# Linear attention and two MLPs on one core: q times kv in the four quarters of the PE array, maximum of k on POOL

## The chip, the cores and the metric

The kernel runs as one program on one core of a Trainium2 chip. The metric is the device time of one execution in microseconds (us). The engines are named as the profile names them: PE is the matrix engine (its weight loads stand apart as PEld), DVE the vector engine, ACT the scalar engine, POOL the general engine, SP the engine whose queue issues all transfers of this kernel.

## What is computed

The cut reference; there are 8 batches of 8 heads, 576 tokens each, head size 64, so 4608 tokens of 512 numbers enter the MLPs.

```python
q_s = exp(q - max(q, axis=-1)); q_s = q_s / (sum(q_s, axis=-1) + 1e-09)
k_s = exp(k - max(k, axis=2));  k_s = k_s / (sum(k_s, axis=2) + 1e-09)   # axis 2: tokens
kv  = einsum('bhsd,bhse->bhde', k_s, v)                # 64 x 64 for each head
x   = einsum('bhsd,bhde->bhse', q_s, kv)               # then heads side by side
x   = relu(x @ w_in)**2 @ w_out                        # 512 -> 2048 -> 512
out = (sigmoid(x @ w_gate) * (x @ w_val)) @ w_out2     # 512 -> 1536 -> 512
```

## The kernel before

All numbers are float32. The products of the MLPs are made of three float32r matmuls each (`mm3`, lines 216 to 219: high by high, high by low, low by high); these three lines are most of PE's work. Blocks 0 and 1 of 512 tokens go through the first MLP in the plain form (`conv_stage`), while the weights are read, split and stored; the later blocks go in pairs, with seven products in place of eight (`plan_seven`), through `in_stage` (first MLP) and `gate_stage` (second MLP).

The attention runs beside the MLPs, as small pieces between the matmuls of a stage. It handles two heads at a time, so there are 4 head pairs `p`. Its work has two parts.

For each batch `b` and pair `p` (`plan_k`): `k` and `v` are loaded with the tokens on the partitions (5 groups of 128). DVE takes the maximum over the 5 groups (`k_max`). What is left is a maximum over 128 partitions. It is made in four steps: PE transposes the 128 x 128 tile (`k_turn`, line 404), DVE reduces it to a column (`k_diag`, line 410), ACT puts the column on a diagonal (`k_put`, line 415), and PE multiplies ones by the diagonal, so that every partition has the row of maxima in PSUM (`k_all`, line 420). DVE subtracts it (`k_sub`, line 425), ACT takes the exponential (`k_exp`, line 429), PE multiplies by `v` and by a column of ones (`k_mm`, line 443: for each group and head a matmul of 128 rows and 64 columns of the array, so the two heads take the two column halves), DVE makes the reciprocal (`k_rec`), and ACT copies the two scaled 64 x 64 blocks onto the diagonal of a 128 x 128 tile `kvf` (`k_copy`, line 460).

For each block `j` of 512 tokens and pair `p` (`plan_q`): `q` is loaded, and its softmax over 64 numbers is made. From block 2 on, `q` lies in memory with blocks of 32 x 32 turned, a maximum or sum over 64 is put together with a small PE matmul (`q_swap`, line 502), and DVE turns the blocks (`q_turn`). Then PE multiplies by `kvf` (`q_mm`, line 571): one matmul over all 128 rows and columns for each batch that the block touches (one or two, `segs`). Each float32 matmul stands as two instructions in the trace. ACT copies the result out of PSUM (`x_copy`).

PSUM has 8 banks: 6 belong to the MLPs (`bank0` to `bank5`), 2 to the attention (the tag `pa`). `k_turn` takes one of them and `k_copy` gives it back; `q_swap` and `q_mm` take one each.

The order of every engine's instructions is fixed before the run. `Plan.trace` is a small simulator: each operation has a key (its wanted time), a cost on an engine, the operations it comes after, the buffers it takes and gives, and some have a `slack` that offers them later than they are ready. An engine takes the ready operation of the lowest key, and its instructions are issued in that order. A result is taken to be usable 0.15 us after its end on DVE, ACT and POOL, 0.2 us on PE. The attention's PE steps of blocks and batches above 3 have a slack of 2.5 us, those below none. Each engine then runs its list in order and waits on semaphores, so an operation that takes longer than its cost in the plan holds up what stands behind it on the engines that wait.

`plan_blocks` lays the attention of blocks 2 and 3 beside the plain stage of block 1, that of blocks 4 and 5 beside the first `in_stage`, that of 6 and 7 beside the second `gate_stage`, and that of block 8 beside the third `in_stage`.

Of the kernel before, what the change touches and what calls it, by code (L numbers as in the profile page):

```python
# [10 lines left out]
F32 = mybir.dt.float32  # L11
# [4 lines left out]
AF = mybir.ActivationFunctionType  # L16
# [7 lines left out]
DMA, PE, ACT, DVE, POOL, FREE = "DMA PE ACT DVE POOL FREE".split()  # L24
# [5 lines left out]
class Plan:  # L30
# [13 lines left out]
    def add(self, key, engines, name, fn, *args, after=(), take=(), give=(), slack=0.0):  # L44
        n = len(self.ops)
        assert name not in self.names, name
        self.names[name] = n
        self.ops.append((key, n, engines, name, fn, args, tuple(after), tuple(take), tuple(give), slack))
# [95 lines left out]
def attention_mlp_mlp(  # L144
# [20 lines left out]
    nc = tc.nc  # L165
    NB, NP, _, N = q.shape
    NBATCH, _, _, RK, D2 = k.shape
    D = D2 // 2
    NT, DM = out.shape
    S = NT // NBATCH  # L170
# [3 lines left out]
    F2 = w_out2.shape[0]  # L174
    wide = w_in.dtype == I64

    SIZES = {"X": 14, "W": 10, "S": 6, "f": 19, "x": 8, "q": 3, "a": 6, "w": 5, "k": 2, "v": 2, "km": 1, "kr": 2, "pa": 2, "qm": 4, "qr": 4}
    cst = ctx.enter_context(tc.tile_pool(name="cst", bufs=1))
    p4 = ctx.enter_context(tc.tile_pool(name="p4", bufs=1))
    p2 = ctx.enter_context(tc.tile_pool(name="p2", bufs=1))  # L180
# [10 lines left out]
    kvf = [[cst.tile([128, 128], F32, name=f"kv{a}{p}") for p in range(NP)] for a in range(2)]  # L191

    vts = [cst.tile([128, RK, 2 * D + 3], F32, name=f"vt{i}") for i in range(SIZES["v"])]
    banks = [pu.tile([128, N], F32, name=f"bank{i}") for i in range(6)]

    plan = Plan(SIZES)
    add = plan.add
# [12 lines left out]
    def hi_of(dst, src):  # L210
        nc.scalar.activation(out=dst, in_=src, func=AF.Copy)  # L211
# [158 lines left out]
    kmx = {}  # L370
    kps = {}
# [45 lines left out]

    def k_all(b, p):

        nc.tensor.matmul(kps[b, p][:, KM0:KM0 + 2 * D], ones, kmx.pop((b, p)), start=True, stop=True)  # L420

    def k_sub(b, p):
        kt = kt_t[b, p]
        mx = kps[b, p][:, KM0:KM0 + 2 * D].rearrange("p (o c) -> p o c", o=1)
        nc.vector.tensor_tensor(out=kt, in0=kt, in1=mx.to_broadcast([128, RK, 2 * D]), op=ALU.subtract)

    def k_exp(b, p):
# [2 lines left out]

    def k_mm(b, p):
        kt, vt = kt_t.pop((b, p)), vt_t.pop((b, p))
        ps = kps[b, p]
        for r in range(RK):
            if b == 0:
                nc.tensor.matmul(ps[:, 0:2 * D + 1], kt[:, r, :], vt[:, r, 0:2 * D + 1], start=(r == 0), stop=(r == RK - 1))  # L436
                continue

            for h in range(2):
                rows = slice(D * h, D * h + D)  # L440
                c = (D + 1) * h
                o = D * (1 - h)
                nc.tensor.matmul(  # L443
                    ps[rows, o:o + D + 1], kt[:, r, rows], vt[:, r, c:c + D + 1],
                    start=(r == 0), stop=(r == RK - 1), skip_group_check=True,
                )
# [8 lines left out]
    def k_copy(b, p):  # L455
        ps, ri = kps.pop((b, p)), kmx.pop((b, p))
        for h in range(2):
            s = slice(D * h, D * h + D)
            c = slice((D + 1) * (1 - h), (D + 1) * (1 - h) + D) if b else s
            nc.scalar.activation(out=kvf[b % 2][p][s, s], in_=ps[s, c], func=AF.Copy, scale=ri[s])  # L460

    def segs(j):
        done = 0
        while done < N:
            b, s = divmod(j * N + done, S)
            c = min(N - done, S - s)
            yield slice(done, done + c), b
            done += c
# [8 lines left out]

    def q_load(j, p):
        t = tile2("q", "qt")
        nc.sync.dma_start(out=t, in_=q[j, p])  # L480
        q_t[j, p] = t

    def qu_cols(j):
# [83 lines left out]
    def q_mm(j, p):  # L567
        t = q_ps.pop((j, p))
        ps = pa.tile([128, N], F32, tag="pa", name="xps")
        for e, b in segs(j):  # L570
            nc.tensor.matmul(ps[:, e], kvf[b % 2][p], t[:, e], start=True, stop=True)  # L571
        q_ps[j, p] = ps
# [10 lines left out]

    def x_copy(j, p):
        t = tile2("x", "xf")
        hi_of(t, q_ps.pop((j, p)))
        x_t[j, p] = t


# [5 lines left out]
    def plan_k(b, p, key, step, wait=()):  # L595
        n = (b, p)
        big = ("W", "W") if b == 0 else ("k", "v")
        bank = [] if b == 0 else ["pa"]
        add(key - 5 if b else p, {DMA: 0.92}, ("kt",) + n, k_load, b, p, after=wait, take=big[:1])
        add(key - 4 if b else p + 4, {DMA: 0.92}, ("vt",) + n, v_load, b, p, after=wait, take=big[1:])  # L600
        add(key, {DVE: 1.02}, ("kmx",) + n, k_max, b, p, after=[("kt",) + n], take=["km"])
        add(key + 0.5 * step, {PE: 0.3}, ("kt2",) + n, k_turn, b, p, after=[("kmx",) + n], take=bank, slack=slack(b))
        add(key + step, {DVE: 0.29}, ("kdr",) + n, k_diag, b, p, after=[("kt2",) + n])
        add(key + 1.2 * step, {ACT: 0.33}, ("kdg",) + n, k_put, b, p, after=[("kdr",) + n])
        add(key + 1.5 * step, {PE: 0.4}, ("kgm",) + n, k_all, b, p, after=[("kdg",) + n], give=["km"], slack=slack(b))
        add(key + 2 * step, {DVE: 0.85}, ("ks",) + n, k_sub, b, p, after=[("kgm",) + n])
        add(key + 3 * step, {ACT: 0.75}, ("ke",) + n, k_exp, b, p, after=[("ks",) + n])
        add(key + 4 * step, {PE: 0.8 if b else 1.3}, ("kp",) + n, k_mm, b, p, after=[("ke",) + n, ("vt",) + n], give=big, slack=slack(b))
        add(key + 5 * step, {DVE: 0.31}, ("kr",) + n, k_rec, b, p, after=[("kp",) + n], take=["kr"])
        add(  # L610
            key + 6 * step, {ACT: 0.65}, ("kv",) + n, k_copy, b, p,
            after=[("kr",) + n] + (kv_users[b - 2, p] or [("kv", b - 2, p)] if b > 1 else []), give=["kr"] + bank,
        )

    def plan_q(j, p, key, step, qmul):
        n = (j, p)
        pe = j < NPE
        add(key - 5 if j else p + 0.1, {DMA: 0.73}, ("qt",) + n, q_load, j, p, after=x_before.get(j, []), take=["q"])
        add(key, {DVE: 0.69}, ("qa",) + n, q_red, j, p, ALU.max, "qm", after=[("qt",) + n], take=["qm"])
        if not pe:  # L620
            add(key + 0.3 * step, {PE: 0.15}, ("qaw",) + n, q_swap, j, p, after=[("qa",) + n], take=["pa"], slack=slack(j))
        if j == JACT:
            add(key + 0.5 * step, {DVE: 0.15}, ("qs",) + n, q_neg, j, p, after=[("qa",) + n])
        else:
            add(key + 0.5 * step, {DVE: 0.7 if pe else 0.86}, ("qs",) + n, q_sub, j, p, after=[("qa" if pe else "qaw",) + n], give=["qm"] if pe else ["qm", "pa"])
        add(key + step, {ACT: 2.4 if j == JACT else 0.63}, ("qe",) + n, q_exp, j, p, after=[("qs",) + n], give=["qm"] if j == JACT else [])
        add(key + 2 * step, {DVE: 0.69}, ("qb",) + n, q_red, j, p, ALU.add, "qr", after=[("qe",) + n], take=["qr"])
        if not pe:
            add(key + 2.3 * step, {PE: 0.15}, ("qbw",) + n, q_swap, j, p, after=[("qb",) + n], take=["pa"], slack=slack(j))
        add(key + 2.5 * step, {DVE: 0.36 if pe else 0.58}, ("qr",) + n, q_sum, j, p, after=[("qb" if pe else "qbw",) + n], give=[] if pe else ["pa"])  # L630
        if j == JACT:
            qmul = {ACT: 2.4}
        add(key + 3 * step, qmul, ("qm",) + n, q_mul, j, p, CHOSEN, after=[("qr",) + n], give=["qr"])
        if pe:
            add(key + 4 * step, {PE: 0.5}, ("qT",) + n, q_turn_pe, j, p, after=[("qm",) + n], take=["pa"], give=["q"], slack=slack(j))
        else:
            add(key + 4 * step, {DVE: 0.72}, ("qT",) + n, q_turn, j, p, after=[("qm",) + n], take=["a"], give=["q"])
        if pe:
            add(key + 5 * step, {ACT: 0.6}, ("qh",) + n, q_copy, j, p, after=[("qT",) + n], take=["a"], give=["pa"])
        bs = [b for _, b in segs(j)]  # L640
        add(
            key + 7 * step, {PE: 1.0}, ("xp",) + n, q_mm, j, p, after=[("qh" if pe else "qT",) + n] + [("kv", b, p) for b in bs],
            take=["pa"], give=["a"], slack=slack(j),
        )
        for b in bs:
            kv_users[b, p].append(("xp",) + n)
        if pe:
            add(key + 8 * step, {ACT: 0.6}, ("xh",) + n, x_hi, j, p, after=[("xp",) + n], take=["SX"[j]])
            add(key + 9 * step, {DVE: 0.7}, ("x",) + n, x_lo, j, p, after=[("xh",) + n], give=["pa"])
            return  # L650
        add(key + 8 * step, {ACT: 0.6}, ("x",) + n, x_copy, j, p, after=[("xp",) + n], take=["x"], give=["pa"])

# [623 lines left out]
```

## Time and profile before

| | |
|---|---|
| median of 3 runs | 1712.5 us (1712.0 to 1712.92) |
| the profiled execution | 1716.37 us, its span 1714.6 us |
| PE busy | 1661.7 us (97% of the span) |
| DVE busy | 1138.8 us (66%) |
| ACT busy | 939.6 us (55%) |
| POOL busy | 2.4 us, 19 instructions |
| bytes moved | 443.32 MB, 259 GB/s in the mean |

The span runs from the first to the last instruction; the profiled time has 1.8 us around it. Matmuls overlap in PE, so PE's busy share says little about how near it is to its peak; the distance between the starts of consecutive matmuls tells what each one costs.

### The profile page before, as it was taken

The page shows a single profiled execution, that of the slowest core. Times are in us where ns is not written, and L with a number is a line of the kernel's source. Part 1 is how long each engine was busy: PE and PEld are TensorE (multiplying, and loading weights), DVE is VectorE, ACT ScalarE, POOL GpSimd, SP SyncE. Part 2 cuts the span into 40 slices and gives each one's busy share as a digit, 9 for nine tenths or more (in the row PEclk, how much of TensorE's full clock was granted, in tenths as well). Part 3 has the DMA queues.
Part 4 walks back from the last instruction along what each step waited for, and adds up shares of the span by engine and source line. Part 5 has one row for each costly group of instructions (what it writes and reads, how often), then busy time and mean ns, then how long its engine had stood idle before and what let it go on. Part 6 is the DMA issues. An engine that isn't in the chain of part 4 may idle for free.

```text
span 1714.6 us, 25673 instructions
## 1 busy us (share of the span) xinstructions
PE 1661.7 (97%) x9404; PEld 1427.6 (83%) x9404; DVE 1138.8 (66%) x2157; ACT 939.6 (55%) x1748; POOL 2.4 (0%) x19
## 2 busy tenths in 40 slices
PE   5898999999999999999999999999999999999999
PEld 4676687788787887889888998888998899889999
DVE  8999678888865687487466974353364494448456
ACT  7688568658473755355467645363443453335344
POOL 0000000000000000000000000000000000000000
PEclk9999999999999999999999999999999999999999
DMA  8787797978697979976766573557777567655797
GB/s 307 267 319 284 266 339 262 325 276 324 230 341 266 359 265 364 332 230 197 246 216 202 177 242 131 196 197 268 279 293 243 194 209 227 204 195 181 237 383 270
DMA packets 163486, 443.32 MB, mean 259 GB/s; under 512 B 15648, under 2 KB 45856, under 8 KB 163360
## 3 DMA queue, kind: packets, MB, share of 16 engines
q1 hardware_dynamic: 163360, 441.68, 74.1%
q8 instruction: 75, 1.23, 0.3%
q14 instruction: 51, 0.42, 0.1%
HBM read 357.20 MB, written 84.41 MB: 258 GB/s over the span
## 4 chain that ended last, share of the span: by engine, by line
PE 86%; DMA 6%; DVE 5%; ACT 2%; SPq 1%; issue 1%; ACTq 0%
PE bank L217 27%; PE bank L218 27%; PE bank L219 27%; DMA w_gv<-whl 1%; PE xps L571 1%; PE kps L443 1%; DMA ws<-w_in 1%; DMA wraw<-in_moe_w_val_dram 1%; DVE whl L214 1%; DVE wf L271 1%; DMA wraw<-in_moe_w_gate_dram 1%; DVE wf L278 1%; DMA ws<-w_gv 0%; PE qsw L502 0%; PE bank L436 0%
## 5 line engine op out<-in xcount | busy, mean ns | idle before, releaser
L217 PE MATMUL bank<-bX,ws 128*128 128x512 f32 (+1 forms) x1288 | 480.4, 373 | 7.3 <-DMA ws<-w_in 6.2
L219 PE MATMUL bank<-bX,ws 128*128 128x512 f32 (+1 forms) x1288 | 473.7, 368 | 0.0
L218 PE MATMUL bank<-bX,ws 128*128 128x512 f32 (+1 forms) x1288 | 473.5, 368 | 0.0
L731 DVE TENSOR_TENSOR s<-s,bank 128x512 f32<-128x512 f32 (+1 forms) x303 | 189.6, 631 | 213.5 <-PE bank L219 172.9
L211 ACT ACTIVATE s<-bank 128x512 f32<-128x512 f32 (+1 forms) x303 | 164.9, 553 | 218.3 <-PE bank L219 201.1
L217 PEld LDWEIGHTS bank<-bX,ws 128*128 128x128 f32 x1288 | 244.4, 190 | 47.0 <-DMA ws<-w_in 6.7
L219 PEld LDWEIGHTS bank<-bX,ws 128*128 128x128 f32 x1288 | 243.9, 189 | 40.5
L218 PEld LDWEIGHTS bank<-bX,ws 128*128 128x128 f32 x1288 | 244.2, 190 | 37.4 <-issue 0.5
L211 ACT ACTIVATE bS<-s 128x512 fp32r<-128x512 f32 (+1 forms) x306 | 176.0, 582 | 158.8 <-PE bank L219 144.2
L214 DVE TENSOR_TENSOR bS<-s,bS 128x512 fp32r<-128x512 f32 (+1 forms) x306 | 190.5, 630 | 82.5 <-ACT bS L211 77.8
L217 PE MATMUL bank<-ws,bS 128*128 128x256 f32 x756 | 214.6, 284 | 0.0
L219 PE MATMUL bank<-ws,bS 128*128 128x256 f32 x756 | 214.0, 283 | 0.0
L218 PE MATMUL bank<-ws,bS 128*128 128x256 f32 x756 | 213.9, 283 | 0.0
L217 PE MATMUL bank<-bS,ws 128*128 128x512 f32 (+1 forms) x512 | 189.3, 370 | 2.3 <-DMA ws<-w_out 2.3
L219 PE MATMUL bank<-bS,ws 128*128 128x512 f32 (+1 forms) x512 | 186.3, 364 | 0.0
L218 PE MATMUL bank<-bS,ws 128*128 128x512 f32 (+1 forms) x512 | 186.2, 364 | 0.0
L217 PEld LDWEIGHTS bank<-ws,bS 128*128 128x128 f32 x756 | 145.0, 192 | 0.8
L218 PEld LDWEIGHTS bank<-ws,bS 128*128 128x128 f32 x756 | 145.0, 192 | 0.7
L219 PEld LDWEIGHTS bank<-ws,bS 128*128 128x128 f32 x756 | 145.0, 192 | 0.0
L750 ACT ACTIVATE s<-s 128x512 f32<-128x512 f32 (+1 forms) x120 | 70.3, 588 | 130.2 <-DVE s L731 129.6
L217 PEld LDWEIGHTS bank<-bS,ws 128*128 128x128 f32 x512 | 97.2, 190 | 18.3 <-DMA ws<-w_out 2.7
L219 PEld LDWEIGHTS bank<-bS,ws 128*128 128x128 f32 x512 | 96.9, 189 | 15.4
(124 smaller groups left out, 2195.8 us busy)
## 6 DMA issues: line engine op xcount, KB each, us to landing
ws<-w_gv SPq DMA_DIRECT2D x210, 512.0 KB, 4.5
ws<-w_out SPq DMA_DIRECT2D x185, 512.0 KB, 4.3
ws<-w_in SPq DMA_DIRECT2D x128, 512.0 KB, 5.9
w_gv<-whl SPq DMA_DIRECT2D x42, 512.0 KB, 5.6
w_out<-whl SPq DMA_DIRECT2D x37, 512.0 KB, 5.1
w_in<-whl SPq DMA_DIRECT2D x32, 512.0 KB, 4.4
wraw<-in_moe_w_out_dram SPq DMA_DIRECT2D x28, 512.0 KB, 5.9
vt<-in_v_dram SPq DMA_DIRECT2D x32, 325.0 KB, 5.6
```

The source lines that it names most:

```text
L211: nc.scalar.activation(out=dst, in_=src, func=AF.Copy)
L214: by_name[engine].tensor_tensor(out=dst, in0=src, in1=hi.bitcast(F32), op=ALU.subtract)
L217: nc.tensor.matmul(ps, ah, bh, start=first, stop=False, skip_group_check=True)
L218: nc.tensor.matmul(ps, ah, bl, start=False, stop=False, skip_group_check=True)
L219: nc.tensor.matmul(ps, al, bh, start=False, stop=last, skip_group_check=True)
L271: nc.vector.scalar_tensor_tensor(out=w, in0=high, scalar=-0x40000000, in1=w, op0=ALU.bitwise_and, op1=ALU.bitwise_or)
L278: by_name[engine].tensor_tensor(out=w, in0=w, in1=low, op=ALU.add)
L443: nc.tensor.matmul(ps[rows, o:o + D + 1], kt[:, r, rows], vt[:, r, c:c + D + 1], start=(r == 0), stop=(r == RK - 1), skip_group_check=True,)
L571: nc.tensor.matmul(ps[:, e], kvf[b % 2][p], t[:, e], start=True, stop=True)
L731: nc.vector.tensor_tensor(out=t, in0=t, in1=banks[pr[b]][:, 0:n], op=ALU.add)
L750: nc.scalar.activation(out=t, in_=t, func=AF.Sigmoid)
```

## The change

From batch 2 on, `k_turn`, `k_diag`, `k_put` and the matmul of `k_all` are replaced by one POOL instruction, `partition_all_reduce`, that reads the 128 x 128 tile of maxima and writes the maximum over the partitions into all partitions of a tile `kgm` in SBUF; `k_sub` reads that. The PSUM bank of a batch is now taken at `k_mm` and no longer at `k_turn`.

From block 2 on, `q_mm` no longer multiplies by the 128 x 128 tile with two blocks of zeros. The 512 tokens are taken in two halves. The second half is loaded with the two heads exchanged on the partitions, by two more transfers. Each 64 x 64 quarter of the array then has work of its own: quarters on the diagonal take the first half, those off it the second, with `kvx`, a copy of `kv` at the other head's partitions, made by two more ACT copies in `k_copy`. The two row halves write to two PSUM banks, so `q_mm` takes both banks of `pa`, and `x_copy` becomes four ACT copies of 64 partitions by 256 columns. Some costs in the plan change too.

```diff
 def k_all(b, p):
+    if b > 1:
+        gm = sp.tile([128, 1, 2 * D], F32, tag="kgm", name="kgm", bufs=SIZES["kg"])
+        nc.gpsimd.partition_all_reduce(
+            gm.rearrange("p o c -> p (o c)"), kmx[b, p][0], 128, bass.bass_isa.ReduceOp.max
+        )
+        kmx[b, p] = gm
+        return
 def k_mm(b, p):
+    if b > 1:
+        kps[b, p] = pa.tile([128, N], F32, tag="pa", name="kps")
 def k_copy(b, p):
         nc.scalar.activation(out=kvf[b % 2][p][s, s], in_=ps[s, c], func=AF.Copy, scale=ri[s])
+        if b:
+            other = slice(D * (1 - h), D * (1 - h) + D)
+            nc.scalar.activation(out=kvx[b % 2][p][other], in_=ps[s, c], func=AF.Copy, scale=ri[s])
 def q_load(j, p):
+        nc.sync.dma_start(out=t[:, 0:N // 2], in_=q[j, p][:, 0:N // 2])
+        for h in range(2):
+            nc.sync.dma_start(out=t[D * h:D * h + D, N // 2:N], in_=q[j, p][D * (1 - h):D * (1 - h) + D, N // 2:N])
 def q_mm(j, p):
+        two = (ps, pa.tile([128, N], F32, tag="pa", name="xps"))
+        for e, b in segs(j):
+            for half in range(2):
+                c = slice(max(e.start, half * (N // 2)), min(e.stop, (half + 1) * (N // 2)))
+                if c.start >= c.stop:
+                    continue
+                for r in range(2):
+                    h = r ^ half
+                    rows, cols = slice(D * r, D * r + D), slice(D * h, D * h + D)
+                    kv = kvx[b % 2][p][rows] if half else kvf[b % 2][p][rows, rows]
+                    nc.tensor.matmul(two[r][cols, c], kv, t[rows, c], start=True, stop=True, skip_group_check=True)
 def x_copy(j, p):
-    hi_of(t, q_ps.pop((j, p)))
+    for half in range(2):
+        c = slice(half * (N // 2), (half + 1) * (N // 2))
+        for r in range(2):
+            h = r ^ half
+            hi_of(t[D * h:D * h + D, c], two[r][D * h:D * h + D, c])
 ...
+            add(key + 0.5 * step, {POOL: 1.0}, ("kgm",) + n, k_all, b, p, after=[("kmx",) + n], take=["kg"], give=["km"])
...
-        add(key + 4 * step, {PE: 0.8 if b else 1.3}, ("kp",) + n, k_mm, b, p, after=[("ke",) + n, ("vt",) + n], give=big, slack=slack(b))
+        add(key + 4 * step, {PE: 0.95 if b else 1.2}, ("kp",) + n, k_mm, b, p, after=[("ke",) + n, ("vt",) + n], take=bank if b > 1 else [], give=big, slack=slack(b))
...
-            key + 6 * step, {ACT: 0.65}, ("kv",) + n, k_copy, b, p,
+            key + 6 * step, {ACT: 1.25 if b else 0.65}, ("kv",) + n, k_copy, b, p,
...
-            key + 7 * step, {PE: 1.0}, ("xp",) + n, q_mm, j, p, after=[("qh" if pe else "qT",) + n] + [("kv", b, p) for b in bs],
-            take=["pa"], give=["a"], slack=slack(j),
+            key + 7 * step, {PE: 0.9 if pe else 0.6}, ("xp",) + n, q_mm, j, p, after=[("qh" if pe else "qT",) + n] + [("kv", b, p) for b in bs],
+            take=["pa"] if pe else ["pa", "pa"], give=["a"], slack=slack(j),
...
-        add(key + 8 * step, {ACT: 0.6}, ("x",) + n, x_copy, j, p, after=[("xp",) + n], take=["x"], give=["pa"])
+        add(key + 8 * step, {ACT: 1.4}, ("x",) + n, x_copy, j, p, after=[("xp",) + n], take=["x"], give=["pa", "pa"])
```

## Rows read from the trace of the kernel before

**Rows 1.** The page's chain that ended last, by engine.
```profile
PE 86%; DMA 6%; DVE 5%; ACT 2%; SPq 1%; issue 1%; ACTq 0%
```
**Rows 2.** Busy time by stretch: its bounds, length, busy us and instructions.
```profile
150.00:300.00 150.00, 144.96 (x802) 116.14 (x801) 121.61 (x260) 102.26 (x193) 0.00 (x0) 0.99 0.80 283
300.00:420.00 120.00, 118.20 (x648) 96.50 (x647) 97.92 (x208) 84.94 (x158) 0.00 (x0) 0.99 0.89 317
420.00:470.00 50.00, 47.24 (x208) 38.55 (x206) 43.30 (x74) 27.03 (x48) 0.00 (x0) 1.00 0.65 219
820.00:980.00 160.00, 159.90 (x969) 134.91 (x968) 110.51 (x223) 99.28 (x154) 0.00 (x0) 1.00 0.64 207
```
**Rows 3.** Timeline of PE around one `k_turn` and one `k_all`: start, us, instruction.
```profile
173.87 0.39 PE L219 MATMUL bank<-x,ws 128*128 128x512 f32 x1
174.10 0.27 PE L404 MATMUL kps<-ident,kmx 128*128 128x128 f32 x1
...
174.44 0.39 PE L218 MATMUL bank<-x,ws 128*128 128x512 f32 x1
174.67 0.40 PE L219 MATMUL bank<-x,ws 128*128 128x512 f32 x1
...
230.53 0.40 PE L219 MATMUL bank<-x,ws 128*128 128x512 f32 x1
230.76 0.39 PE L420 MATMUL kps<-kmx,ones 128*128 128x128 f32 x2
...
231.22 0.39 PE L218 MATMUL bank<-x,ws 128*128 128x512 f32 x1
```
**Rows 4.** Timeline of PE around one `q_mm` and one `k_mm`.
```profile
169.25 0.39 PE L219 MATMUL bank<-x,ws 128*128 128x512 f32 x1
169.57 0.80 PE L443 MATMUL kps<-vt,kt 128*64 128x65 f32 x20
...
170.64 0.39 PE L218 MATMUL bank<-g0hl,ws 128*128 128x512 f32 x1
...
222.00 0.40 PE L219 MATMUL bank<-x,ws 128*128 128x512 f32 x1
222.24 1.03 PE L571 MATMUL xps<-qtr,kv 128*128 128x128 f32 x4
...
223.34 0.39 PE L218 MATMUL bank<-x,ws 128*128 128x512 f32 x1
```
**Rows 5.** Who waited for whom on PE: us in total, times, longest.
```profile
PE kps L443 <- ACT kt L429: 4.0, 3, 1.9
```
**Rows 6.** The chain that ended last, around 462 us: start, us, what.
```profile
461.68 0.60 DVE bX L214
...
464.62 6.93 DMA ws<-w_in
```
**Rows 7.** Groups on POOL: busy us, mean ns, idle before.
```profile
masks.py:199 POOL TENSOR_SCALAR_AFFINE_SELECT ident<-ident 128x128 f32<-128x128 f32 x1 | 0.3, 292 | 0.1
...
L1265 POOL MEMSET const-float32-1.0<- 128x1 f32 x1 | 0.1, 98 | 0.0
```
**Rows 8.** One group on DVE, by form.
```profile
L410 DVE TENSOR_REDUCE km<-kps 128x1 f32<-128x128 f32 x28 | 7.9, 281 | 3.3 <-PE kps L404 3.3
```
**Rows 9.** Groups on ACT, by form.
```profile
L211 ACT ACTIVATE s<-bank 128x256 f32<-128x256 f32 x60 | 22.9, 382 | 46.4 <-PE bank L219 29.8 <-DVE xp L867 16.4
L460 ACT ACTIVATE kv<-kps,kri 64x64 f32<-64x64 f32 x56 | 17.1, 306 | 13.2 <-DVE kri L452 12.9
L211 ACT ACTIVATE xf<-xps 128x512 f32<-128x512 f32 x28 | 16.7, 596 | 25.9 <-PE xps L571 25.9
L415 ACT ACTIVATE kmx<-ident,km 128x128 f32<-128x128 f32 x32 | 12.7, 396 | 9.2 <-DVE km L410 8.7
```
**Rows 10.** Timeline of SP's queue, one load of q.
```profile
362.78 0.34 SPq L480 DMA_DIRECT2D qt<-in_q_dram  x1
```
**Rows 11.** What SP's queue waited for: us in total, times, longest.
```profile
SPq L301 <- PE bank L219: 747.3, 382, 8.0
```

More of the change, by code (lines that the diff above doesn't have):

```diff
@@ L175, in attention_mlp_mlp @@
     wide = w_in.dtype == I64
-    SIZES = {"X": 14, "W": 10, "S": 6, "f": 19, "x": 8, "q": 3, "a": 6, "w": 5, "k": 2, "v": 2, "km": 1, "kr": 2, "pa": 2, "qm": 4, "qr": 4}
+    SIZES = {"X": 14, "W": 10, "S": 6, "f": 19, "x": 8, "q": 3, "a": 6, "w": 5, "k": 2, "v": 2, "km": 1, "kr": 2, "pa": 2, "qm": 4, "qr": 4, "kg": 2}
     cst = ctx.enter_context(tc.tile_pool(name="cst", bufs=1))
@@ L193, in attention_mlp_mlp @@
     vts = [cst.tile([128, RK, 2 * D + 3], F32, name=f"vt{i}") for i in range(SIZES["v"])]
+    kvx = [[cst.tile([128, D], F32, name=f"kx{a}{p}") for p in range(NP)] for a in range(2)]
     banks = [pu.tile([128, N], F32, name=f"bank{i}") for i in range(6)]
@@ L423, in k_sub @@
         kt = kt_t[b, p]
-        mx = kps[b, p][:, KM0:KM0 + 2 * D].rearrange("p (o c) -> p o c", o=1)
+        mx = kmx.pop((b, p)) if b > 1 else kps[b, p][:, KM0:KM0 + 2 * D].rearrange("p (o c) -> p o c", o=1)
         nc.vector.tensor_tensor(out=kt, in0=kt, in1=mx.to_broadcast([128, RK, 2 * D]), op=ALU.subtract)
@@ L479, in q_load @@
         t = tile2("q", "qt")
-        nc.sync.dma_start(out=t, in_=q[j, p])
+        if j < NPE:
+            nc.sync.dma_start(out=t, in_=q[j, p])
+        else:
+            nc.sync.dma_start(out=t[:, 0:N // 2], in_=q[j, p][:, 0:N // 2])
+            for h in range(2):
+                nc.sync.dma_start(out=t[D * h:D * h + D, N // 2:N], in_=q[j, p][D * (1 - h):D * (1 - h) + D, N // 2:N])
         q_t[j, p] = t
@@ L569, in q_mm @@
         ps = pa.tile([128, N], F32, tag="pa", name="xps")
+        if j >= NPE:
+            two = (ps, pa.tile([128, N], F32, tag="pa", name="xps"))
[9 more added lines that the diff above has]
+                        nc.tensor.matmul(two[r][cols, c], kv, t[rows, c], start=True, stop=True, skip_group_check=True)
+            q_ps[j, p] = two
+            return
         for e, b in segs(j):
@@ L585, in x_copy @@
         t = tile2("x", "xf")
-        hi_of(t, q_ps.pop((j, p)))
+        two = q_ps.pop((j, p))
+        for half in range(2):
[3 more added lines that the diff above has]
+                hi_of(t[D * h:D * h + D, c], two[r][D * h:D * h + D, c])
         x_t[j, p] = t
@@ L601, in plan_k @@
         add(key, {DVE: 1.02}, ("kmx",) + n, k_max, b, p, after=[("kt",) + n], take=["km"])
[L602 to L606, printed above, removed]
+        if b > 1:
+            add(key + 0.5 * step, {POOL: 1.0}, ("kgm",) + n, k_all, b, p, after=[("kmx",) + n], take=["kg"], give=["km"])
+        else:
+            add(key + 0.5 * step, {PE: 0.13}, ("kt2",) + n, k_turn, b, p, after=[("kmx",) + n], take=bank)
+            add(key + step, {DVE: 0.29}, ("kdr",) + n, k_diag, b, p, after=[("kt2",) + n])
+            add(key + 1.2 * step, {ACT: 0.33}, ("kdg",) + n, k_put, b, p, after=[("kdr",) + n])
+            add(key + 1.5 * step, {PE: 0.24}, ("kgm",) + n, k_all, b, p, after=[("kdg",) + n], give=["km"])
+        add(key + 2 * step, {DVE: 0.85}, ("ks",) + n, k_sub, b, p, after=[("kgm",) + n], give=["kg"] if b > 1 else [])
         add(key + 3 * step, {ACT: 0.75}, ("ke",) + n, k_exp, b, p, after=[("ks",) + n])
-        add(key + 4 * step, {PE: 0.8 if b else 1.3}, ("kp",) + n, k_mm, b, p, after=[("ke",) + n, ("vt",) + n], give=big, slack=slack(b))
+        add(key + 4 * step, {PE: 0.95 if b else 1.2}, ("kp",) + n, k_mm, b, p, after=[("ke",) + n, ("vt",) + n], take=bank if b > 1 else [], give=big, slack=slack(b))
         add(key + 5 * step, {DVE: 0.31}, ("kr",) + n, k_rec, b, p, after=[("kp",) + n], take=["kr"])
         add(
-            key + 6 * step, {ACT: 0.65}, ("kv",) + n, k_copy, b, p,
+            key + 6 * step, {ACT: 1.25 if b else 0.65}, ("kv",) + n, k_copy, b, p,
             after=[("kr",) + n] + (kv_users[b - 2, p] or [("kv", b - 2, p)] if b > 1 else []), give=["kr"] + bank,
```

## The prediction

> **What bounds the kernel now.** First the chain of work that ended last: PE has 86% of it [rows 1]. Then the stretches in which the changed work lies. From 300 to 420 and from 820 to 980 us PE is busy for 118.2 of 120 and 159.9 of 160 us, while DVE idles 22 and 49 us and ACT 35 and 61 [rows 2]: there a microsecond of matmuls saved is one of the span. From 420 to 470 it is not so: the chain runs without a gap along DVE to 462 us and then through one load of weights that PE waits for [rows 6], and DVE is busy for 43.3 of 50 us [rows 2]. What PE gains before that load counts only as far as DVE comes earlier too.
>
> A matmul's own duration says little, since they overlap; I take the distance from the last main matmul ahead of a piece to the second one behind it, less two common distances of 0.23 us (174.44 to 174.67, [rows 3]). So `k_turn` costs 0.57 - 0.46 = 0.11 us and `k_all` 0.69 - 0.46 = 0.23 us [rows 3]; `k_mm` costs 1.39 - 0.46 = 0.93 us and `q_mm` 1.34 - 0.46 = 0.88 us [rows 4].
>
> **The maximum of k.** The batches 2 to 7 with 4 pairs are 24 cases. PE loses 24 x (0.11 + 0.23) = 8.2 us of work. DVE loses `k_diag`, 24 x 0.281 = 6.7 us [rows 8], ACT loses `k_put`, 24 x 0.396 = 9.5 us [rows 9].
>
> Added is one POOL instruction, of which the trace has no example. POOL's one pass over a 128 x 128 tile took 0.292 us, and its instruction for a single column 0.098 us [rows 7]. Below, it costs one pass, 0.29 us. Above, it goes column by column, 128 x 0.098 = 12.5 us. A fold over 128 partitions is 7 halvings; with the spreading that is 8 passes, 2.3 us. The row it is nearest to is the pass over the same tile, so I look between 0.29 and 2.3 us and take 1.5, since the fold can't be a single pass but its steps can overlap. Both ends stay for the range. POOL is otherwise empty (its 2.4 us are set-up), so its own time costs nothing. What counts is who waits: `k_sub` stands in DVE's queue at the place where the plan has it ready, 1.0 + 0.15 us behind `k_max`. If POOL is later, DVE stops there, and behind it stand the additions that free the banks of the MLPs and the low halves that PE wants next. In batches 4 to 7 the slack of 2.5 us in front of `k_mm` and DVE's idle time take 0.35 us. Batches 2 and 3 have no slack, and PE already waited there for `k_exp`, 4.0 us in three waits [rows 5]; so I count 8 x 0.35 = +2.8 us. At 0.29 us this term is 0; at 2.3 us it is 8 x 1.15 = +9.2.
>
> **The quarters.** Blocks 2 to 8 with 4 pairs are 28 cases. Before, 2 instructions on each of 512 columns took 0.88 us, 0.86 ns for a column of one instruction. `k_mm` shows what a divided array does: 20 instructions of 65 columns are 1300, at 0.86 ns one after another 1.12 us, and it took 0.93. With two column halves at work together they take 0.56, and 0.37 us are left over: 0.32 us instead of 0.23 lie before the first, and the first main matmul behind it comes late too [rows 4]. I read that as the price of going into a divided array and back. The new `q_mm` has 2 instructions on 256 columns in each of four quarters. If the four run together, 0.44 us; if only two do, as seen, 0.88. With 0.37 on top that is 0.81 or 1.25. Without it, 0.44. So a case changes by -0.44 (four together, entry free), -0.07 (four, entry as in `k_mm`) or +0.37 (two, entry as in `k_mm`): -12.3, -2.0 or +10.4 us for 28. The nearest row for the entry is `k_mm`'s. For four at once no row speaks, but in `k_mm` the two halves take different data from the same partitions at the same time, and nothing of the diagonal quarters is shared; I take four together, -2.0, and keep both ends.
>
> The Trainium skill (TensorEngine Tiling (Array Packing), Theoretical Speedup and Key Properties) counts 64 x 64 as four independent tiles, but says that a change of mode drains the engine. By its speedup alone the sum would have -12.3 here; the row of `k_mm` shows the drain's side, and gives -2.0.
>
> **The copies on ACT.** `k_copy` makes two more copies of 64 x 64, 28 x 2 x 0.306 = +17.1 us. `x_copy` makes four of 256 columns where one of 512 took 0.596; the nearest row has 128 x 256 at 0.382, so 28 x (4 x 0.382 - 0.596) = +26.1 us [rows 9]. With `k_put` gone ACT has +33.7 us. I cost it at nothing: ACT idles 61 us in 820 to 980 and 35 in 300 to 420 [rows 2], and that idle time hides it. What stands behind an `x_copy` on ACT are the copies that free MLP banks, later by 0.93 us; were PE to wait for each, it would be 28 x 0.93 = 26 us.
>
> **Loads and banks.** `q` comes by three transfers, not one: 56 more issues of 0.34 us [rows 10], 19 us in SP's queue. That queue waits 747 us for PE to release weight buffers [rows 11], which hides them. The last third is issued 0.68 us later; without the 5 us of lead in its key, DVE would wait 28 x 0.68 = 19 us for it. `q_mm` now wants both attention banks at once, so `q_swap` and `k_mm` of another pair stand back until `x_copy` is done, 1.5 us; against that a batch holds its bank only from `k_mm` on, no longer over `k_diag` to `k_exp`. There are 8 cases in the 160 us from 820 to 980, 20 us each, so I cost it at nothing; at its worst a case is 1.5 us late.
>
> **The sum.** PE's work: -8.2 - 2.0 = -10.2. Of it 16 of 24 cases of k and 16 of 28 of q lie before 470 us: 5.5 + 1.1 = 6.6. There DVE sets the pace, and DVE is relieved of 16 x 0.281 = 4.5 us, so 2.1 of the 6.6 do not come through. POOL's wait adds 2.8. Together -10.2 + 2.1 + 2.8 = -5.3. The profiled execution took 1716.37 us, its span 1714.6 and 1.8 around it; 1716.4 - 5.3 = 1711.1, and it was 3.9 us over the median of the runs. Against the median it is 1712.5 - 5.3 = 1707.2; I say 1707.
>
> **The rivals.**
>
> *The entry is cheap.* Four quarters together and no 0.37 us: -12.3 in place of -2.0, so 1707.2 - 10.3 = 1697. For it: pieces often stand next to each other, and one entry can serve two. Against it: each `k_mm` alone pays it.
>
> *Two quarters at a time.* +10.4 in place of -2.0: 1707.2 + 12.4 = 1719.6. For it: no row has more than two tiles at work. Without the quarters the sum is -5.3 + 2.0 = -3.3, and 3.3 / 28 = 0.12: it decides from 0.88 + 0.12 - 0.37 = 0.63 us of array time a case on.
>
> *POOL is late.* Without the POOL term the sum is -8.1; each microsecond beyond 1.15 costs 8 us in batches 2 and 3, and beyond 1.15 + 2.5 another 16 in batches 4 to 7. It turns the sign at 1.15 + 1.0 = 2.2 us, near the 8 passes. At 5 us: 8 x 3.85 + 16 x 1.35 - 8.1 = +44, 1757. Against it: DVE's idle time takes a part.
>
> *POOL goes column by column.* At 12.5 us: 8 x 11.35 + 16 x 8.85 - 8.1 = +224, 1937. Only the one-column row speaks for it. The Trainium skill (GPSIMD Engine Reference, Performance versus the Vector engine) gives 247,699 ns for a reduction of [128, 2048] over the partitions; an estimate from that for 128 columns is 15.5 us. No run here shows it, and it is another instruction.
>
> *Nothing comes of it.* The order of the whole list shifts with the costs, and the gain goes into a longer wait for the load at 464 us: 1712.
>
> **Chances.** The forecast 0.45, the cheap entry 0.17, two quarters 0.13, POOL late 0.15, column by column 0.05, nothing 0.05. Faster or slower means by over 0.2%, 3.4 us, which is about what a measurement of this kernel can tell from no change. The forecast's own range is 1699 to 1714, from no wait for POOL and half of the entry (-2.8 - 5.1) to 2.3 us on POOL (+6.4); some 0.33 of its 0.45 lies below 1709.1. So faster 0.33 + 0.17 = 0.50, same 0.12 + 0.05 = 0.17, slower 0.13 + 0.15 + 0.05 = 0.33. The range from 1696 to 1725 holds the forecast, the cheap entry, two quarters, nothing, and the beginning of a late POOL; what it leaves out is the later POOL and the far end.
>
> **What the profile after would show.** If right: `k_turn` and `k_all` gone from PE for batches 2 to 7; `q_mm` at 0.8 us between main matmuls, with starts in fours; the POOL instruction at 0.3 to 2.3 us; ACT some 34 us busier, DVE some 7 less; DVE's wait for POOL at `k_sub` a few microseconds in all. Wrong would make it: starts of `q_mm` in twos, a long wait of `k_sub` for POOL with waits of PE behind it, new waits of PE for ACT's copies or for the bank pair, or a longer wait for the load near 464 us.

## The result and the profile after

The changed kernel takes 1726.62 us (median of 4 runs, 1722.75 to 1728.26), the kernel before 1712.71 us in the same measurement. The ratio is 1.0070, 95% interval [1.0056, 1.0084]: slower, where a gain of 5 us was forecast. The profiled execution took 1722.75 us, its span is 1721.0 us, 6.4 longer than before.

**The new pieces do what they should.** Busy time by stretch in the changed kernel, with the columns of [rows 2]:

```profile
0.00:30.00 30.00, 9.40 (x41) 6.92 (x42) 16.62 (x41) 11.91 (x22) 2.36 (x19) 0.97 0.63 224
...
150.00:300.00 150.00, 138.73 (x815) 109.12 (x814) 111.46 (x234) 105.87 (x226) 8.02 (x9) 0.97 0.82 280
300.00:420.00 120.00, 116.31 (x687) 91.34 (x687) 98.96 (x209) 94.77 (x192) 5.81 (x7) 0.99 0.83 302
420.00:470.00 50.00, 50.00 (x231) 40.96 (x231) 41.73 (x74) 36.14 (x66) 0.00 (x0) 1.00 0.63 232
...
820.00:980.00 160.00, 160.00 (x1018) 134.51 (x1018) 100.78 (x198) 97.34 (x173) 4.38 (x5) 1.00 0.67 214
```

From 820 to 980 us PE is as full as in [rows 2], and there the change gains (below). The price of each piece comes from its groups on POOL and ACT, from the waits of DVE and PE, and from the timeline of PE around one `q_mm`:

```profile
L423 POOL PARTITION_ALL_REDUCE kgm<-kmx x24 | 20.6, 859 | 901.4 <-DVE kmx L400 730.8 <-DVE kri L461 145.0 <-DVE qst L529 25.6
```
```profile
L212 ACT ACTIVATE xf<-xps 64x256 f32<-64x256 f32 x112 | 39.3, 375 | 26.6 <-PE xps L601 25.5
L473 ACT ACTIVATE kx<-kps,kri 64x64 f32<-64x64 f32 x56 | 17.3, 310 | 0.7
```
```profile
DVE kt L433 <- POOL kgm L423: 2.1, 3, 0.9
```
```profile
846.30 0.39 PE L220 MATMUL bank<-bX,ws 128*128 128x512 f32 x1
846.61 0.43 PE L601 MATMUL xps<-qtr,kv 64*64 64x256 f32 x2
846.63 0.43 PE L601 MATMUL xps<-qtr,kx 64*64 64x128 f32 x4
846.88 0.38 PE L601 MATMUL xps<-qtr,kv 64*64 64x256 f32 x2
846.90 0.39 PE L601 MATMUL xps<-qtr,kx 64*64 64x128 f32 x4
847.21 0.50 PE L218 MATMUL bank<-bX,ws 128*128 128x512 f32 x1
847.55 0.40 PE L219 MATMUL bank<-bX,ws 128*128 128x512 f32 x1
```

The reduction takes 0.86 us in the mean (0.70 to 1.26 in the trace), and DVE waits 2.1 us for it in all. A `q_mm` costs 847.55 - 846.30 - 0.46 = 0.79 us, measured as in [rows 4]. In the 26 of the 28 cases that stand alone between main matmuls at full clock the median is 0.79 too; before, it was 0.88 in 20 such cases. The timeline merges instructions of one form. Taken singly, this `q_mm` starts with four within 0.02 us (846.614 to 846.634), two on `kv` and two on `kx`. Two quarters at a time would need 0.88 us at the forecast's 0.86 ns a column; from the first start to the last end it is 847.28 - 846.61 = 0.67 us. So more than two quarters work at once, and the starts in fours were the sign of the forecast. The Trainium skill (TensorEngine Tiling (Array Packing), Available Configurations and Key Properties) has four independent tiles at 64 x 64 and says that a change of mode drains the engine, without a time for it. The row agrees, and a `q_mm` keeps 0.79 of its 0.88 us.

**Where the time went.** The n-th of the 8436 main matmuls of `mm3` is compared in both kernels. The table is worked out from the start times in both traces:

| start before, us | 35.3 | 79.7 | 125.5 | 199.9 | 231.9 | 316.8 | 476.9 | 811.0 | 993.6 | 1710.4 (the last) |
|---|---|---|---|---|---|---|---|---|---|---|
| start after minus before | +7.6 | +5.9 | +12.1 | +3.7 | +10.6 | +12.8 | +12.6 | +11.6 | +6.7 | +6.5 |

There are two losses: 7.6 us before the first main matmul, and a second one between 80 and 317 us; then comes a gain of 5 between 811 and 994 us. The second loss begins between 80 and 126 us, where only batch 1, block 1 and the plain stage run: none of the new pieces is there yet. The small difference at 200 us also holds attention pieces that stand at other places in the two lists; what of the second loss lasts is read below, from two kernels with the same pieces.

**The first loss.** Timeline of POOL at the start of the kernel before, then that of the changed one; last, PE's first instruction after the change:

```profile
0.73 0.20 POOL masks.py:197 MEMSET ident<- 128x128 f32 x1 [0.29 <-POOLq L1265]
1.00 0.29 POOL masks.py:199 TENSOR_SCALAR_AFFINE_SELECT ident<-ident 128x128 f32<-128x128 f32 x1
```
```profile
0.72 0.20 POOL masks.py:197 MEMSET ident<- 128x128 f32 x1 [0.29 <-POOLq L1307]
10.07 0.28 POOL masks.py:199 TENSOR_SCALAR_AFFINE_SELECT ident<-ident 128x128 f32<-128x128 f32 x1 [9.15 <-issue]
```
```profile
10.39 1.44 DVE L1249 COPY swap<-ident 128x64 f32<-128x64 f32 x2 [10.39 <-POOL ident masks.py:199]
```
```profile
12.65 0.45 PE L405 MATMUL bank<-ident,kmx 128*128 128x128 f32 x1 [12.65 <-DVE kmx L400]
```

POOL stands still for 9.15 us with nothing in the trace that it waits for ("issue"), in the middle of making the identity. DVE's queue has a copy of the identity at its head and stops; behind it stand the maxima that PE's first transpose needs. PE starts at 12.65 us; before, it started at 4.85. The first reduction comes only at 157 us. That POOL's code is loaded in this gap is a reading: no row names it. What the traces show is where the gap stands: in all four kernels that have both a reduction and the identity on POOL (9.15 to 9.76 us), and in none without a reduction.

**The second loss.** What PE waited for from 78 to 132 us, and its timeline there, both after the change:

```profile
PE bank L218 <- ACT g0hl L212: 3.9, 2, 2.8
PE kps L428 <- ACT kmx L416: 3.2, 1, 3.2
```
```profile
105.36 0.39 PE L219 MATMUL bank<-x,whl 128*128 128x512 f32 x1
105.58 0.39 PE L220 MATMUL bank<-x,whl 128*128 128x512 f32 x1
109.17 0.49 PE L428 MATMUL kps<-kmx,ones 128*128 128x128 f32 x2 [3.20 <-ACT kmx L416]
109.42 0.48 PE L218 MATMUL bank<-g0hl,whl 128*128 128x512 f32 x1
...
110.89 0.63 PE L220 MATMUL bank<-g0hl,whl 128*128 128x512 f32 x1
111.31 0.63 PE L218 MATMUL bank<-g0hl,whl 128*128 128x512 f32 x1
...
113.84 0.39 PE L218 MATMUL bank<-x,whl 128*128 128x512 f32 x1
114.07 0.40 PE L219 MATMUL bank<-x,whl 128*128 128x512 f32 x1
```

PE waits 3.20 us at one `k_all` (line 428) of batch 1, whose instructions the change did not touch. Behind it stand the matmuls on `g0hl`. From 110.46 us on, for 3.4 us, they start 0.43 us apart and not 0.23; the granted clock is then the lower level:

```profile
106.00:109.00 3.00, 0.00 (x0) 0.00 (x0) 2.40 (x5) 2.96 (x6) 0.00 (x0) 1.00 0.98 376
109.20:110.40 1.20, 1.20 (x6) 1.06 (x7) 1.20 (x3) 1.20 (x3) 0.00 (x0) 0.99 0.84 335
110.50:114.00 3.50, 3.50 (x10) 2.79 (x9) 3.36 (x9) 3.50 (x10) 0.00 (x0) 0.53 0.59 240
```

PE is idle from 106 to 109 us, does six instructions at full clock, and has 0.53 (near 1.2 of 2.4 GHz) from 110.5 to 114. Eight distances of 0.43 in place of 0.23 are 1.6 us on top of the wait.

### The profile page after: what moved, and what is told of

It reads as the page before. It is cut to its first block, busy times and chain, and to the rows that moved or that the text cites. A ratio compares the mean times of both kernels' runs of the same rounds, so it can differ in the third digit from the quotient of the medians.

```text
span 1721.0 us, 26211 instructions
## 1 busy us (share of the span) xinstructions
PE 1650.7 (96%) x9532; PEld 1412.7 (82%) x9532; DVE 1132.1 (66%) x2130; ACT 973.4 (57%) x1869; POOL 23.0 (1%) x43
## 3 DMA queue, kind: packets, MB, share of 16 engines
q8 instruction: 76, 1.25, 0.3%
## 4 chain that ended last, share of the span: by engine, by line
PE 84%; DMA 6%; DVE 6%; ACT 2%; issue 2%; SPq 0%; POOL 0%; ACTq 0%; DVEq 0%; POOLq 0%
PE bank L218 27%; PE bank L219 27%; PE bank L220 27%; DMA w_gv<-whl 1%; DMA wraw<-in_moe_w_out_dram 1%; PE kps L453 1%; PE xps L601 1%; DMA ws<-w_in 1%; DMA wraw<-in_moe_w_gate_dram 1%; DVE whl L215 1%; DMA w_in<-whl 1%; DVE wf L272 1%; DVE wf L279 1%; PE qsw L521 0%; DVE bX L215 0%
```

## The experiments

Two theories came out of this. The load: the start waits for POOL's code. The order: the lowered costs of batches and blocks 0 and 1 in the plan give the lists another order, and PE then waits at pieces that come late. The rival to both is that the new pieces themselves hold PE up. The kernels below take them apart; each is compared with the kernel before on the same chip. Where an expectation gives a theory a letter, it says itself what the theory is. The expectations name runs by number: e1 is the load by itself, e2 the changed kernel with the identity on DVE, e3 the quarters alone, e5 and e6 the two kernels with the identity on DVE and the old first costs (both parts, and POOL alone).

**The load by itself.** The kernel before with one reduction whose result nobody uses.

```diff
+    spare = cst.tile([128, 128], F32, name="spare")
+    nc.gpsimd.partition_all_reduce(spare, ident, 128, bass.bass_isa.ReduceOp.max)
     for names in (fetched, xorder, sorder):
```

> The kernel before with one POOL reduction over the partitions, of the identity into a tile that nobody reads, behind the set-up. Theory A (the code that POOL loads before its first instructions sets the start back): POOL stands still for about 9 us before it fills the identity, PE's first instruction comes at about 12.6 us instead of 4.85, and the time is 1712.7 + 7.6 = 1720. Rival B (the loss comes from the new order or from the new pieces): the start is as before, 1712.7.

Ratio 1.0045 [1.0029, 1.0061]. Its POOL timeline:

```profile
10.19 0.28 POOL masks.py:199 TENSOR_SCALAR_AFFINE_SELECT ident<-ident 128x128 f32<-128x128 f32 x1 [9.26 <-issue]
...
18.21 0.72 POOL L1217 PARTITION_ALL_REDUCE spare<-ident  x1 [5.89 <-issue]
```

The main matmuls are 7.0 us late at the first and 7.1 at 1000 us: the late start is not made up. Nobody waits for this reduction, so the loss is that of the gap ahead of the identity.

**The identity on DVE.** In the changed kernel, and as a control in the kernel before, twelve small DVE instructions make the identity. The lines left out make a row of 1 to 32 by five doublings, and its transpose as a column.

```diff
-    make_identity(nc, ident)
+    nc.vector.memset(ident, 0.0)
...
+    for i in range(4):
+        b32 = slice(32 * i, 32 * i + 32)
+        nc.vector.tensor_scalar(out=ident[b32, b32], in0=row[b32], scalar1=col[b32, 0:1], scalar2=None, op0=ALU.is_equal)
```

> The changed kernel with the identity made by DVE (12 small instructions) instead of POOL, so that nothing early waits for POOL's load. Theory A: PE's first instruction is back near 5 us and 7.6 us come back: 1726.6 - 7.6 = 1719. If the load is the whole loss: 1712 or less. Rival B: the start is not the cause, 1726.

> The kernel before with the identity by DVE and nothing else: the control for e2, e5 and e6. PE's first main matmul in those came 1.3 to 2.9 us earlier than in the kernel before. If that is worth its face: ratio 0.9985 to 0.999; if the later waits take it back: 1.000.

The changed kernel comes to 1.0022 [1.0010, 1.0033], the control to 1.0000 [0.9988, 1.0012]. So the gap at the start holds as a cause, and 0.0048 of the 0.0070 goes with it; the control shows no gain from the new identity by itself. The changed kernel now starts 2.0 us early, but is 7.1 late at 126 us: the second loss stands, with the same wait of 3.2 us.

**Each part alone.** The kernel before with only the quarters and their costs, and with only the maximum on POOL and its costs (and the load).

> The kernel before with only the second part of the change: the four quarters, the second tile of kv, the three loads of q, the four copies, and their costs in the plan; the maximum of k is made as before. No POOL reduction, so no load. By the term of the prediction -2.0: 1710.7. If the copies on ACT or the two banks at once hold PE up: above 1716.

> The kernel before with only the first part of the change: the maximum of k by POOL from batch 2 on, and its costs in the plan. Theory A: the load sets the start back by 7.6 us, and PE is relieved of 24 x 0.34 = 8.2 us of which at least the 8 cases behind 470 us come through, 2.7: between 1712.7 + 7.6 - 8.2 = 1712 and 1712.7 + 7.6 - 2.7 = 1718. Rival B (this part's order loses besides): 1720 or more.

The quarters alone give 1.0102 [1.0084, 1.0119], a loss where -2.0 us were forecast; POOL alone gives 1.0016 [1.0000, 1.0033], inside the range of theory A. The quarters alone lose 11.5 us between 275 and 317 us. In the changed kernel that stretch loses 2.4. So the loss of the quarters alone is not a part of the change's loss; what it is was followed up below.

**The order of the first batches.** The old costs of the untouched batches and blocks 0 and 1 are put back; no instruction changes, only the order of the lists. The four costs, cut out of their lines:

```diff
-            {PE: 0.13}, ("kt2",)   {PE: 0.24}, ("kgm",)   {PE: 0.95 if b else 1.2}, ("kp",)   {PE: 0.9 if pe else 0.6}, ("xp",)
+            {PE: 0.3}, ("kt2",)    {PE: 0.4}, ("kgm",)    {PE: (0.95 if b > 1 else 0.8) if b else 1.3}, ("kp",)    {PE: 1.0 if pe else 0.6}, ("xp",)
```

With the identity on DVE:

> The changed kernel with the identity by DVE and, for batches 0 and 1 and blocks 0 and 1, the costs that the plan had before (0.3, 0.4, 1.3 or 0.8, 1.0). Theory C (the new costs of the first blocks, whose work is not changed, give an order that stands worse on the chip): the 7.7 us that e2 lost between 80 and 132 us come back, the ratio goes from 1.0022 to about 0.998. Rival D (those us belong to the new pieces): as e2, 1.002.

The same with only the maximum on POOL and no quarters:

> Only the maximum of k on POOL, with the identity by DVE and the old costs for batches 0 and 1: the first part of the change without the load at the start and without the order of the first blocks. By the terms of the prediction -8.2 less what DVE's pace holds back, and -2 from the earlier start: ratio between 0.994 and 0.998. If POOL's instruction holds DVE and PE up: 1.000 or more.

The changed kernel with its load, only the costs put back:

> The changed kernel with the old costs for batches 0 and 1 and blocks 0 and 1, the identity on POOL as changed, so with the load at the start. If the two causes add: e5 plus the load, 0.9961 + 0.0045 = 1.0006. If the order alone decides and the load is covered by other waits: 0.996.

The first gives 0.9961 [0.9947, 0.9975], 1707.14 us against 1713.93; the second 0.9961 [0.9947, 0.9975] as well; the third 0.9999 [0.9988, 1.0010]. So the order holds too: with both parts in it costs 0.006 to 0.007, whether the load is there or not, and the load 0.004 to 0.005. Without both the change gains what it was meant to gain: -6.7 us, between -9.1 and -4.3, where -5.3 was forecast.

Where the order costs this time, the third kernel shows. It has the instructions of the changed kernel, the load too, and only the old costs. The changed kernel is behind it by:

| start before, us | 79.7 | 125.5 | 199.9 | 231.9 | 275.0 | 316.8 | 476.9 | 1710.4 |
|---|---|---|---|---|---|---|---|---|
| changed minus old first costs, us | -1.5 | +3.9 | -0.8 | +1.9 | +4.4 | +8.7 | +7.5 | +8.1 |

At 199.9 both have started the same 298 matmuls of the attention, and nothing is left of the 3.9 us. What lasts is lost between 200 and 317 us. With the identity on DVE the same comparison loses 1.6 us between 80 and 200 us and 12.1 from there to 317, of 13.0 at the end. Busy time from the main matmul of 199.9 to that of 316.8 in the changed kernel, then with the old first costs:

```profile
203.60:329.60 126.00, 112.92 (x650) 88.42 (x649) 94.16 (x196) 90.26 (x184) 6.11 (x7) 0.96 0.84 293
```
```profile
204.40:320.90 116.50, 109.15 (x650) 85.03 (x649) 90.00 (x191) 88.50 (x182) 5.59 (x7) 1.00 0.88 308
```

The same 650 instructions of PE take 126.0 and 116.5 us. PE is idle for 13.1 and 7.4 us of it, and its granted clock is 0.96 and 1.00. Among PE's waits in the changed kernel are these, all between 200 and 320 us:

```profile
PE qsw L521 <- ACT xf L212: 3.5, 2, 2.3
PE xps L601 <- DVE qtr L571: 3.3, 1, 3.3
PE kps L453 <- ACT xf L212: 1.8, 1, 1.8
```

With the old first costs PE waits 1.0 us for `q_turn` (`qtr`) and never for `x_copy` (`xf`). Each side of this comparison is one trace.

**Which way, and which cost.** The new first costs in the kernel before; the same moved the other way (0.47, 0.56, 1.4 and 0.65); and in the changed kernel with the identity on DVE, the old costs of the batches alone, then of `k_turn` and `k_all` alone, then of `k_mm` alone.

> The kernel before with nothing changed but three costs of the plan for batches 0 and 1 (0.13, 0.24, 1.2 or 0.95). The instructions are the same, only their order differs. Theory C: 4 to 8 us are lost between 80 and 135 us, ratio 1.002 to 1.005. Rival D: 1.000.

> The kernel before with the same three costs of batches 0 and 1 moved as far the other way (0.47, 0.56, 1.4 or 0.65). Theory C1 (lower costs of PE there put its steps too early, so the direction matters): 1.000 or less. Theory C2 (the order of the first 480 us is one good draw and any new draw loses): 1.005 or more.

> The changed kernel with the identity on DVE and the old costs for the untouched batches 0 and 1 (k_turn 0.3, k_all 0.4, k_mm 1.3 and 0.8), while q_mm of blocks 0 and 1 keeps its new cost of 0.9. If the three costs of the batches are what lost 0.6% in the changed kernel: ratio near 0.996. If it was the cost of q_mm of blocks 0 and 1: near 1.002.

> The changed kernel with the identity on DVE; of the lowered costs only those of k_turn (0.3) and k_all (0.4) are put back, k_mm keeps the new 1.2 and 0.95 in batches 0 and 1. In the changed kernel PE stands 3.2 us at one k_all of batch 1, which the kernel before does not. If the costs of k_turn and k_all put it there too early: that wait is gone and the ratio is near 0.996. If k_mm's cost did it: the wait stays and the ratio is near 1.002.

> The counterpart: only k_mm's old costs (1.3 in batch 0, 0.8 in batch 1) are put back, k_turn and k_all keep 0.13 and 0.24. If k_turn and k_all are the cause: the wait of 3.2 us stays, ratio near 1.002. If k_mm is: no such wait, ratio near 0.996.

Lowered: 1.0112 [1.0091, 1.0132], more than the 1.002 to 1.005 expected. Moved the other way: 0.9999 [0.9985, 1.0012]. So not every other order is worse. With the batches' three old costs 0.9962 [0.9947, 0.9977], so `q_mm`'s cost in blocks 0 and 1 does nothing that can be told. But neither half of them is enough: 1.0031 [1.0012, 1.0049] with `k_turn` and `k_all`, 1.0015 [1.0002, 1.0027] with `k_mm`. Both expectations of the last pair missed their 0.996; the order turns on the costs together.

The wait at `k_all` marks the order. PE's 3.2 us there, in batch 1, stand in six kernels, all that have a new first cost of the batches in their plan: the changed one, the one with the identity on DVE, POOL alone, the lowered costs alone, and the two halves. The kernel before and all others, with the old or the raised costs, have no such wait. But it is not the whole loss, and may be little of it: in POOL alone, which has the wait, load and order together cost 0.0055 (1.0016 against 0.9961), hardly more than the load by itself. With the batches' old costs back, the same place on PE's timeline is:

```profile
99.11 0.27 PE L405 MATMUL kps<-ident,kmx 128*128 128x128 f32 x1
100.30 0.50 PE L218 MATMUL bank<-g0hl,whl 128*128 128x512 f32 x1 [0.92 <-ACT g0hl L212]
...
103.54 0.40 PE L220 MATMUL bank<-g0hl,whl 128*128 128x512 f32 x1
103.78 0.38 PE L428 MATMUL kps<-kmx,ones 128*128 128x128 f32 x2
```

Here twelve matmuls on `g0hl` stand between `k_turn` and `k_all`, and cover `k_diag` and `k_put`; nothing waits at 103.78. In the changed kernel `k_all` stands ahead of those matmuls.

**What the quarters alone ran into.** The plan of the quarters (their costs, two banks at once) with the old pieces; the quarters' pieces with the old costs and still two banks; then two banks and nothing else; then the costs and nothing else.

```diff
-            take=["pa"], give=["a"], slack=slack(j),
+            take=["pa"] if pe else ["pa", "pa"], give=["a"], slack=slack(j),
...
-        add(key + 8 * step, {ACT: 0.6}, ("x",) + n, x_copy, j, p, after=[("xp",) + n], take=["x"], give=["pa"])
+        add(key + 8 * step, {ACT: 0.6}, ("x",) + n, x_copy, j, p, after=[("xp",) + n], take=["x"], give=["pa"] if pe else ["pa", "pa"])
```

> The kernel before with the costs and the two banks that the change puts into the plan for the copies of kv, q times kv and the copies of x, but with the old pieces: again the same instructions in another order. Theory C (the loss of e3, 1.010, is one of order): 1.005 to 1.010. Rival D (it is one of the four copies, three loads and the array mode): within 0.998 to 1.002.

> The kernel before with q times kv in four quarters from block 2 on and nothing else, but with the old costs of the pieces in the plan, so that the list keeps an order close to that of before (the two banks are still taken together). Theory (the 1.0102 of the quarters alone came from the order that their costs gave, not from the pieces): ratio 0.998 to 1.002, and no loss of 10 us between 275 and 320 us. Rival (the pieces themselves, or taking two banks at once, hold PE up): ratio near 1.01, with the loss in the same place.

> The kernel before, its pieces and costs unchanged; only its plan lets q_mm of the blocks from 2 on take both attention banks (it writes to one of them) and x_copy give both back. A batch still holds a bank from k_turn to k_copy. Theory D (the loss of the quarters alone came from two banks wanted at once while a batch holds one over its whole chain; the change removes this with its other part, which takes the bank at k_mm only): ratio 1.007 to 1.015, with 10 us or more lost between 275 and 320 us. Rival (the costs order the list worse): ratio 0.998 to 1.003.

> The kernel before with old pieces and the costs of the quarters in the plan (k_copy 1.25, q_mm 0.6, x_copy 1.4), but one bank for q_mm. Theory D: ratio 0.998 to 1.003, as the costs alone do not matter. Rival (costs): ratio near 1.009, as with both banks.

1.0087 [1.0059, 1.0115], 1.0161 [1.0130, 1.0191], 1.0072 [1.0051, 1.0094] and 1.0015 [0.9999, 1.0031]. The second overthrew the theory that the quarters' costs were to blame: with the old ones it was worse. What the three slow ones share is the two banks. Those alone, with every instruction as before, lose 14 us between 126 and 477 us (4.0 early at 126, 9.8 late at 477; at both places as many of the attention's matmuls have started as in the kernel before). Busy time from 275 to 330 us in the kernel before, and with two banks in the plan:

```profile
275.00:330.00 55.00, 53.20 (x270) 43.57 (x269) 47.33 (x99) 46.80 (x88) 0.00 (x0) 0.97 0.81 295
```
```profile
275.00:330.00 55.00, 47.19 (x221) 35.73 (x220) 45.31 (x86) 43.06 (x82) 0.00 (x0) 0.91 0.63 228
```

With two banks in the plan PE is idle for 7.8 of these 55 us, against 1.8 before. The reading is this: as long as a batch holds a bank over its whole chain from `k_turn` to `k_copy`, a piece that wants both banks has no place between two batches, and the list is put in another order. No run shows that step by itself. In the changed kernel a batch takes its bank at `k_mm` only, and two banks cost nothing there that can be told: the kernel with both parts freed and that with POOL alone have the same ratio, 0.9961.

## Why the prediction was wrong

**The maximum of k.** Right in the main. The forecast had 1.5 us for POOL between 0.29 and 2.3; it takes 0.86. DVE's wait was put at 2.8 us and is 2.1 in three waits, the longest 0.9 us. That the two are near is luck: by the forecast's own formula 0.86 us gives no wait, one of the three waits is in batch 7, and in the kernel freed of both losses DVE never waits for POOL. The reading of [rows 5] was wrong in part: two of its three waits (0.5 and 1.7 us, at 130.5 and 145.7 us) are in batch 1, and only that of 1.9 us is in batch 2. DVE is busy for 6.7 us less, as worked out from [rows 8] (1132.1 after, 1138.8 before). POOL late and column by column fall.

**The quarters.** The sizes were right: 0.79 us where 0.81 was worked out with four quarters at work and the entry paid as in `k_mm`. The cheap entry (0.44) and two quarters at a time (1.25) both fall. Between 811 and 994 us the kernel with both parts freed gains 4.9 us on the kernel before and that with POOL alone, freed as well, 3.9. The difference of 1.0 us in these two traces stands for the 8 cases there, for which the forecast has 0.6. Over the whole kernel the quarters give nothing that can be told from zero, nor from the -2.0 forecast.

**ACT's copies, loads and banks.** Costed at nothing, with ACT up by 33.7 us; it is up by 33.8 (973.4 after, 939.6 before), and in the changed kernel PE waits for `x_copy` 5.3 us in three waits (two at `q_swap`, 3.5 us, one at `k_mm`, 1.8, shown above), which the forecast had as an end and not as a term. With the old first costs there is none of these waits left, with the load or without it, so they came with the order. `x_copy`'s copies take 0.375 us, where 0.382 was taken from [rows 9]. That two banks cost nothing is true only beside the other part: by themselves they cost 0.7%. The prediction had the shorter hold of a batch's bank as what makes up for them, and the runs agree with that.

**The step that failed first** is "POOL is otherwise empty (its 2.4 us are set-up), so its own time costs nothing". The row of POOL's set-up [rows 7] was read as busy time only. But the instruction shown there makes the identity, on which the head of DVE's queue and PE's first instruction hang; what comes late there came late for the whole kernel. A price for bringing in a new kind of POOL instruction was not in the sum at all: 0.0045 alone, some 7.7 us.

**The second failed step** is that "some costs in the plan change too" got no term where the pieces themselves stay. It appears only in the rival "nothing comes of it" as a shift of the list with the load at 464 us as its end; the chance given was 0.05. The order did shift, from batch 1 on and not at 464 us, and costs 0.006 to 0.007, more than the gain; most of that is lost between 200 and 317 us. The trace of the kernel before could have shown where it matters: the lists of the first batches have no slack, and PE already waits for `k_exp` in batches 1 and 2 [rows 5].

**The sum.** Forecast for the pieces -5.3 us. Freed of both losses the change measures 0.9961, which is 1713.9 x 0.0039 = -6.7 us. In its trace (a run 1 us under their median) 2.7 us are gained by 80 us with the earlier start, 2.3 between 80 and 811 us and 5.1 behind; the forecast had 1.7 before 470 us and 3.6 behind. Put together, -0.39% for the pieces, +0.38 to +0.48% for the load and +0.60 to +0.71% for the order, against a measured +0.70%.

**What stays open.** Which exchange in the order leads to the waits between 200 and 317 us, and what part the wait at `k_all` has in them. And why lowered costs alone lose 1.1% in the kernel before, when the same costs lose only 0.6% beside the new pieces. The trace shows where: of the 23 us 16.8 go between 200 and 317 us, and between 200 and 335 us PE waits there 6.4 us at `k_mm` for `k_exp`, 5.4 at `q_swap` for `x_copy` and 2.0 at `k_all`; the kernel before has 0.3 us at `k_all` in that stretch and none of the others. Loading the code earlier, with the identity still on POOL, was not tried.

## What to carry to other kernels

A new kind of instruction on a quiet engine can have a price at the very start of the kernel, where set-up work on that engine can be the start of the critical path. Look at what hangs on it before calling it free, and let another engine make what the others wait for at the start. Where a plan orders the queues by costs, a change of costs is a change of the kernel of its own: measure it by itself, and change the costs of the new pieces only. A part that is bad by itself may be harmless beside the other part, which frees the resource that it takes (here a bank), so a change is taken apart both ways before a part is blamed.

## What the runs showed of the hardware

With the reduction in the program and the identity made on POOL, POOL stands still ahead of the identity for 9.15 to 9.76 us, in four kernels, and the trace shows nothing there. Ahead of the reduction itself it stands for 5.89 us in the kernel where nothing else delays it. With no identity made on POOL the first stretch is gone. The Trainium skill (GPSIMD Engine Reference, Instruction dispatch) says that the first call to a freshly loaded kernel pays for bringing its code in, with no instruction to be seen in the profile, and gives 5.95 us; the 5.89 agrees, the 9.15 to 9.76 are longer.

A maximum over 128 partitions of 128 columns takes 0.86 us on POOL, in place of 0.34 us of PE, 0.28 of DVE and 0.40 of ACT.

After 3.2 us without work PE was granted full clock for six instructions, and only then the lower level for some 3.4 us: this stall cost 1.6 us on top of its 3.2.
